# Five of eight sets of weight sums made on VectorE in the last stage, not by accumulating DMAs

## The chip, the cores and the metric

The kernel runs on one core of a Trainium2 chip. The metric is the device time of one execution in microseconds (us). A core has TensorE (PE), VectorE (DVE), ScalarE (ACT), GpSimd (POOL) and SyncE (SP); each works through its own instructions in order. All DMAs are issued here by SP, a few by POOL and ACT, and run on the core's 16 DMA engines.

## The reference

```python
def _moe_ref(x, expert_emb, tau, w1, w2):        # x: 2304 tokens of 512, from the attention
    ...
    for e in range(E):                            # 8 experts, one for each token
        mask = expert_idx == e
        h = np.maximum(x[mask] @ w1[e], 0.0)      # 512 to 1024
        out[mask] = gate_w[mask, None] * (h @ w2[e])
    return out

def _moe2_ref(x, w_in, w_out):                    # w_in 512x2048, w_out 2048x512
    h = x @ w_in
    g = h * (1.0 / (1.0 + np.exp(-h)))
    return g @ w_out
```

An attention (32 pairs of batch and head, 576 tokens each) makes the tokens, a layer of experts follows (`_moe_ref`), and a feed-forward layer with two matrices ends it (`_moe2_ref`). All is fp32.

## The kernel before

PE reads an fp32 matrix as two parts, high and low, so that a product is three matmuls: high by high, high by low, low by high (`three`, lines 798 to 800). The parts are made by a copy on ACT (high) and a subtraction on DVE (low). This goes for weights and for activations.

**The slots.** After the attention come 22 expert slots, each for up to 128 tokens of one expert. SP loads the expert's weights, 4 MB when the expert changes, in pieces of 1536 and 512 KB (`fetch`, line 811, into `raw`). ACT and DVE split them (`split`, lines 847 and 848). PE turns the tokens of the next slot (`xturn`, four transposes into `pxt`, line 868), multiplies (`mm1`, then `mm2` of the slot before) and turns the result (`hturn`; the copies `hh` and `hl`, lines 852 and 855). POOL gathers the tokens of later slots (`gather`, line 833).

**Weight sums.** The last stage multiplies by `w_in` in a scheme of seven products instead of eight for a pair of column tiles q (0 to 7) and a block of 576 tokens. For it each pair needs seven matrices, each 256x128 and held as 128x256: four are tiles of the converted `w_in`, three are sums of these. They lie side by side in DRAM, in `sscr[q]`, [128, 7, 256], 896 KB. The first five pairs' tiles are converted during the attention, the last three during slots 7 to 16, with their loads and stores on POOL's queue (`cload`, `cwork`, `cstore`). `keep_weights` stores a tile, some of it broadcast to several places. Then `add_weights` (line 193) adds one place onto others by an accumulating DMA from DRAM to DRAM on POOL's queue. `ADDS` lists 21 of these: 13 of three places (384 KB) and 8 of one (128 KB). Slot s issues two of them, from slot 8 on. For the last three pairs DVE makes one sum on the way (`both`, line 224), and a store spreads it (line 184).

**The last stage.** It is cut in 32 units u, unit u for pair q = u % 8 and token block u // 8. PE runs in unit u the products 1, 5, then 4 of the unit before, 6, 3 of the unit before, 2 and 7 (`unit`); each is six matmuls of 128x288. Products 1, 6, 7, 4 collect in PSUM bank A, where ACT copies them out (`keep`). Products 5 and 3 collect in bank C and 2 in B, where DVE adds them onto the copied tile (`join`), and SP stores the result (`hstore`, into `hd`). `join(u, 5)` reads bank C before product 3 of u adds to it, so PE waits for it. A dictionary `todo` holds what is done after product n in unit u: `at(u, n, task)`; the order in which it runs is the order on each engine. Before the change:

- `wfetch(q)` loads `sscr[q]` as it is into the low half of the weight tile (SP, line 983): q = 0 to 3 in the last slots into `wb`, 4 and 5 ahead of unit 0 and 6 and 7 in units 1 and 2, into `wbr`. 
- `whigh(q)` (ACT, after product 6 of unit q-2) and `wlow(q)` (DVE, after product 5 of unit q-1) split it. 
- `xfetch`, `xscale` and `xprep` prepare the tokens of the next block from unit 2 on: a load of `yt` (by SP or as a gather by POOL, line 1002), a scale by the gate on DVE for the first two tiles (line 1010), and four transposes on PE (line 1019). The first of them stand after product 1 of units 2 and 3.
- `oload`, `cwork`, `cstore` convert the 16 tiles of `w_out` in units 6 to 24.
- The branch `rest`, for experts with more tokens than the slots hold, stands ahead of unit 5 and is not taken.

A down stage (`w_out`) ends the kernel.

Of the kernel before, what the change touches and what calls it, by code (L numbers as in the profile page):

```python
# [9 lines left out]
F32 = mybir.dt.float32  # L10
# [4 lines left out]
ALU = mybir.AluOpType  # L15
# [4 lines left out]
P = 128  # L20
# [12 lines left out]
NJ = FF2 // P  # L33
TN = 288
NJP = NJ // 2
# [9 lines left out]
CA = 10  # L45
# [3 lines left out]
SQ = [{}, {1: (0, 1), 3: (2, 3), 5: (4,)}, {1: (0, 1), 3: (2, 3), 5: (4,)}, {i: (i,) for i in range(NB)}]  # L49
RANK = (1, 0)  # L50
WARM = (10, 14)
BITS = [-1, 0, 1, 2, 3, 4, 5, 6, 7, 11, 12, 13, 14, 15, 19, 20, 21, 22, 23, 24]
# [14 lines left out]
def moe_kernel(ctx, tc, qk, v, w_phi, emb, tau, w1, w2, win, wout, out):  # L67
    nc = tc.nc
# [9 lines left out]
    yd = dram.tile([NT + 2 * P, DM], F32, name="yd")  # L78
    sscr = [dram.tile([P, 7, 256], F32, name=f"sscr{i}") for i in range(NJP)]
    woscr = [dram.tile([P, 2, DM], F32, name=f"woscr{i}") for i in range(NJP)]  # L80
# [89 lines left out]

    def keep_weights(i, c, rw, dma=nc.sync):
        half, j = divmod(i, NJ)
        q, odd = divmod(j, 2)
        c = c.bitcast(F32)
        if half:
            dma.dma_start(out=woscr[q][:, odd, :], in_=c)
        elif i < CA and odd:
            dma.dma_start(out=sscr[q][:, 6, :], in_=c[:, 0:256])
            dma.dma_start(out=sscr[q][:, 2:6, :], in_=c[:, 256:512].unsqueeze(1).to_broadcast([P, 4, 256]))
        elif odd:  # L180
            both = rw.rearrange("p f t -> p (f t)")[:, 0:256].bitcast(F32)
            dma.dma_start(out=sscr[q][:, 6, :], in_=c[:, 0:256])
            dma.dma_start(out=sscr[q][:, 2, :], in_=c[:, 256:512])
            dma.dma_start(out=sscr[q][:, 3:6, :], in_=both.unsqueeze(1).to_broadcast([P, 3, 256]))
        else:
            dma.dma_start(out=sscr[q][:, 0:2, :], in_=c.rearrange("p (a f) -> p a f", a=2))

    ADDS = [(q, n) for n in (6, 0, 1) for q in range(CA // 2)] + [(5, 0), (6, 0), (5, 1), (7, 0), (6, 1), (7, 1)]

    def add_weights(q, n):  # L190
        a, b = {6: (3, 6), 0: (4, 7), 1: (5, 6)}[n]
        src = sscr[q][:, n:n + 1, :]
        nc.gpsimd.dma_start(out=sscr[q][:, a:b, :], in_=src.to_broadcast([P, b - a, 256]) if b - a > 1 else src,
                            accum_op=ALU.add)

    def narrow(rw, c, eng, i):
# [16 lines left out]
        for f in (shift, scale) if eng is nc.scalar else (scale, shift):  # L213
# [5 lines left out]
                                       op1=ALU.bitwise_xor)  # L219
        if CA <= i < NJ and i % 2:  # L220
            yield
            a, b = c.bitcast(F32)[:, 0:256], c.bitcast(F32)[:, 256:512]
            both = rw.rearrange("p f t -> p (f t)")[:, 0:256].bitcast(F32)
            nc.vector.tensor_tensor(out=both, in0=a, in1=b, op=ALU.add)

    class Convert:
# [13 lines left out]
        def work(self, i):  # L240
            c = self.done(i)
            yield from narrow(self.h[i], c, nc.vector, i)
            self.h[i] = c, self.h[i]

        def store(self, i):
            keep_weights(i, *self.h.pop(i))

# [9 lines left out]
    def phase_all(ctx):  # L257
# [517 lines left out]
        pools = {}  # L775
# [174 lines left out]
        def cstore(i, dma):  # L950
            rw, c, todo = J.pop(i)
            next(todo, None)
            keep_weights(i, c, rw, dma)

# [25 lines left out]
        def wfetch(q):  # L980
            if q < 4:
                wspace(q)
            nc.sync.dma_start(out=W[q][1].bitcast(F32), in_=sscr[q].rearrange("p a f -> p (a f)"))

        def whigh(q):
            nc.scalar.copy(out=W[q][0], in_=W[q][1].bitcast(F32))

        def wlow(q):
            hi, lo = W[q]
            nc.vector.tensor_tensor(out=lo, in0=lo.bitcast(F32), in1=hi.bitcast(F32), op=ALU.subtract)  # L990

# [432 lines left out]
        for s in range(1, NSF + 1):  # L1424
# [9 lines left out]
            if s < NSF:  # L1434
                if s + 2 < NSF:
                    gather(s + 2)
                for q, n in ADDS[max(2 * s - 16, 0):max(2 * s - 14, 0)]:
                    add_weights(q, n)
                for k in range(4):
# [48 lines left out]
            if s == NSF - 1:  # L1488
                xfetch(1, 0)
                xfetch(1, 1)  # L1490
                wfetch(3)
            if s < NSF:
# [15 lines left out]
        def at(u, n, *task):  # L1508
            todo.setdefault((u, n), []).append(task)

        htile(0, (0, 0))
        for q in range(4, NJP):
            wspace(q)
        wfetch(4)
        wfetch(5)
        def plan():
            for q in range(2, NJP):
                at(q - 2, 6, whigh, q)
                at(q - 1, 5, wlow, q)
            at(1, 4, wfetch, 6)  # L1520
            at(2, 4, wfetch, 7)
            for k in range(1, NT // (2 * TN)):
# [13 lines left out]
                for v, n, name in ((7, 5, "T1n"), (7, 6, "T2n"), (7, 2, "B21"), (7, 7, "T3"), (8, 4, "T4"), (8, 3, "B22")):  # L1536
                    at(u + v, n, xsplit, k, name)
            units = [u for u in range(6, 25) if u not in (7, 15, 23)]
            assert len(units) == NJ
# [19 lines left out]
        for u in range(NUNIT):  # L1559
            if u == NJP - 3:  # L1560
                more = nc.values_load(regs[0:1, 2, NSF:NSF + 1], min_val=0, max_val=NT + P)
                with tc.If(more < NT + P):
                    rest()
            unit(u, todo, EARLYP)
# [53 lines left out]
```

## Time and profile before

| | |
|---|---|
| median of 3 runs | 927.96 us (927.53 to 928.4) |
| the profiled execution, whole | 928.01 us |
| its span on the core | 926.3 us |
| PE busy | 900.8 us |
| DVE, ACT, POOL busy | 618.4, 583.1, 267.7 us |

The span goes from the first to the last instruction on the core; 1.7 us of the execution lie around it. An engine is busy while it runs an instruction; in order to see what it waits for in the rest of the time, one reads the list of its waits (for whom, how long, how often) and the timeline, where a wait stands in brackets behind the instruction that ended it.

### The profile page before, as it was taken

How to read it: one execution, taken by the hardware profiler on the slowest of the kernel's cores; microseconds unless marked ns; L12 is line 12 of the kernel's file. 1: busy time of each engine (PE TensorE's matmuls, PEld its weight loads, DVE VectorE, ACT ScalarE, POOL GpSimd, SP SyncE). 2: the span in 40 equal slices, each digit the busy share in tenths (PEclk: the TensorE clock that was granted, in tenths of full speed). 3: DMA queues.
4: the chain of work that ended last, by engine and by line, in shares of the span. 5: the costliest groups of instructions: out<-in, count | busy, mean ns of one | idle time of the engine just before them, and what ended most of it. 6: DMA issues, size and time to landing. Idle time of an engine off the chain costs nothing. (4 is left out here: it accounts for less than half of the span.)

```text
span 926.3 us, 15648 instructions
## 1 busy us (share of the span) xinstructions
PE 900.8 (97%) x5567; PEld 787.3 (85%) x5567; DVE 618.4 (67%) x967; ACT 583.1 (63%) x948; POOL 267.7 (29%) x236
## 2 busy tenths in 40 slices
PE   8999999999999999979999989999999999999996
PEld 6999999987767788858878889999999888888885
DVE  7888898986798999959988857676756122222220
ACT  6877888745978898859888755343456344444331
POOL 6887887712200406416230021101000110000000
PEclk9999999999999999989999999999999999999999
DMA  6455353449455738995698585777776844444420
GB/s 181 111 155 169 93 180 93 112 134 363 159 184 195 252 90 203 356 335 142 179 324 322 190 287 182 232 261 232 241 255 209 209 114 119 120 113 114 119 63 23
DMA packets 136739, 171.69 MB, mean 185 GB/s; under 512 B 34664, under 2 KB 97768, under 8 KB 136656
## 3 DMA queue, kind: packets, MB, share of 16 engines
q1 hardware_dynamic: 124064, 144.06, 48.8%
q0 software_dynamic: 12512, 26.55, 10.9%
q8 instruction: 45, 0.74, 0.3%
q14 instruction: 38, 0.31, 0.1%
q10 hardware_dynamic: 80, 0.03, 0.0%
HBM read 170.87 MB, written 52.04 MB: 241 GB/s over the span
## 5 line engine op out<-in xcount | busy, mean ns | idle before, releaser
L848 DVE TENSOR_TENSOR wl<-raw,wh 128x1024 fp32r<-128x1024 f32 (+1 forms) x166 | 187.7, 1173 | 31.6 <-ACT wh L847 26.8
L847 ACT CAST wh<-raw 128x1024 fp32r<-128x1024 f32 (+1 forms) x166 | 161.4, 1026 | 27.5 <-DMA raw<-w 15.3
L1169 DVE TENSOR_TENSOR hlt<-gt,hlt 128x1024 fp32r<-128x1024 f32 x34 | 41.7, 1226 | 146.4 <-ACT hlt L1168 146.4
L1093 ACT COPY ht<-puA 128x288 f32<-128x288 f32 x128 | 51.0, 400 | 92.4 <-PE puA L800 81.4
L799 PE MATMUL po<-wob,hlt 128*128 128x512 f32 x272 | 108.5, 399 | 0.0
L798 PE MATMUL po<-wob,hlt 128*128 128x512 f32 x272 | 107.2, 394 | 0.0
L800 PE MATMUL po<-wob,hlt 128*128 128x512 f32 x272 | 106.6, 392 | 0.0
L434 POOL TENSOR_TENSOR kl<-ke,kh 128x640 fp32r<-128x640 f32 x52 | 84.1, 1639 | 30.7 <-issue 23.0
L1189 ACT COPY os<-po 128x512 f32<-128x512 f32 x17 | 10.0, 588 | 108.4 <-PE po L800 108.4
L484 PE MATMUL pnx<-kv,qp 128*128 128x73 f32 x640 | 76.6, 275 | 0.0
L484 PEld LDWEIGHTS pnx<-kv,qp 128*128 128x128 f32 x640 | 74.1, 192 | 0.1
L1190 POOL DMA_INDIRECT out<-os,oidx x18 | 17.6, 976 | 179.1 <-ACT os L1189 168.6
L798 PE MATMUL ph<-wh,xh 128*128 128x512 f32 x166 | 67.1, 404 | 0.0
L800 PE MATMUL ph<-wh,xl 128*128 128x512 f32 x166 | 65.1, 392 | 0.8 <-DVE xl L855 0.8
L799 PE MATMUL ph<-wl,xh 128*128 128x512 f32 x166 | 64.7, 390 | 0.0
L1100 DVE TENSOR_TENSOR ht<-puC,ht 128x288 f32<-128x288 f32 x64 | 29.0, 453 | 52.7 <-PE puC L800 39.1
L395 DVE TENSOR_REDUCE m<-pqk 128x10 f32<-128x1280 f32 x32 | 47.5, 1485 | 24.3 <-PE pqk L389 22.9
L798 PEld LDWEIGHTS po<-wob,hlt 128*128 128x128 f32 x272 | 51.0, 188 | 13.3
L800 PEld LDWEIGHTS po<-wob,hlt 128*128 128x128 f32 x272 | 51.1, 188 | 12.3
L419 ACT ACTIVATE ke<-d 128x640 f32<-128x640 f32 x52 | 38.3, 737 | 36.7 <-DVE d L396 36.7
L799 PEld LDWEIGHTS po<-wob,hlt 128*128 128x128 f32 x272 | 51.0, 188 | 11.6
L389 PE MATMUL pqk<-wbd,zh 128*128 128x256 f32 (+1 forms) x320 | 59.0, 283 | 0.8 <-DVE d L396 0.6
(403 smaller groups left out, 2443.8 us busy)
## 6 DMA issues: line engine op xcount, KB each, us to landing
raw<-w SPq DMA_DIRECT2D x44, 1536.0 KB
raw<-w SPq DMA_DIRECT2D x44, 512.0 KB
hd<-ht SPq DMA_DIRECT2D x124, 144.0 KB
gt<-hd SPq DMA_DIRECT2D x15, 1024.0 KB
z<-qk SPq DMA_DIRECT2D x32, 288.0 KB
wo<-wout SPq DMA_DIRECT2D x16, 512.0 KB
yd<-ys SPq DMA_DIRECT2D x23, 256.0 KB
raw<-win SPq DMA_DIRECT2D x10, 512.0 KB
```

What stands on the lines that cost most here:

```text
L389: nc.tensor.matmul(out=pqk[0:r, c * 256:(c + 1) * 256], lhsT=z[:, c * P:c * P + r], rhs=wbd[:, j].rearrange("p h f -> p (h f)"), start=(i ...
L395: nc.vector.tensor_reduce(out=m, in_=pv, axis=AX.X, op=ALU.max, apply_absolute_value=True)
L419: nc.scalar.activation(out=ke, in_=kd, func=AF.Exp, scale=1.0 - 2.0 * s)
L434: nc.gpsimd.tensor_tensor(out=kl[:, :, s, :], in0=st.pop(("ke", g, s)), in1=kh[:, :, s, :].bitcast(F32), op=ALU.subtract)
L484: nc.tensor.matmul(out=pn[:, c, 0:73], lhsT=qp[:, s, c * P:(c + 1) * P], rhs=kv[:, s, 0:73], start=(s == 0), stop=(s == 1))
L798: nc.tensor.matmul(out=o, lhsT=ah, rhs=bh, start=first, stop=False, skip_group_check=more)
L799: nc.tensor.matmul(out=o, lhsT=ah, rhs=bl, start=False, stop=False, skip_group_check=more)
L800: nc.tensor.matmul(out=o, lhsT=al, rhs=bh, start=False, stop=last, skip_group_check=more)
L847: nc.scalar.copy(out=hi[:, 0:n], in_=sl[:, 0:n])
L848: nc.vector.tensor_tensor(out=lo[:, 0:n], in0=sl[:, 0:n], in1=hi[:, 0:n].bitcast(F32), op=ALU.subtract)
L1093: nc.scalar.copy(out=htile(u, at), in_=BK[u, "A"])
L1169: nc.vector.tensor_tensor(out=lo, in0=g, in1=hi.bitcast(F32), op=ALU.subtract)
```

## The change

Pairs 0 to 2 (`QD = 3`) keep their sums in DRAM, by nine accumulating DMAs, one a slot from slot 8 to slot 16. For pairs 3 to 7 only the four tiles are stored ([128, 4, 256], 512 KB, without broadcasts). In units 0 to 4 SP loads them into a tile `ws` in SBUF (two buffers), and DVE makes the sums there with four additions of 128x256 (`wsum`). `whigh` and `wlow` read from `ws` and write the weight tile. `wfetch(3)` leaves the last slots, and `wfetch(4)` and `(5)` leave the place ahead of unit 0. The tiles of `w_out`, which use the same two buffers, are converted in units 8 to 25, and the branch stands ahead of unit 7.

```diff
+QD = 3
...
-    sscr = [dram.tile([P, 7, 256], F32, name=f"sscr{i}") for i in range(NJP)]
+    sscr = [dram.tile([P, 7 if i < QD else 4, 256], F32, name=f"sscr{i}") for i in range(NJP)]
...
-        elif i < CA and odd:
+        elif q >= QD:
+            if odd:
+                dma.dma_start(out=sscr[q][:, 0, :], in_=c[:, 0:256])
+                dma.dma_start(out=sscr[q][:, 3, :], in_=c[:, 256:512])
+            else:
+                dma.dma_start(out=sscr[q][:, 1:3, :], in_=c.rearrange("p (a f) -> p a f", a=2))
+        elif odd:
             dma.dma_start(out=sscr[q][:, 6, :], in_=c[:, 0:256])
             dma.dma_start(out=sscr[q][:, 2:6, :], in_=c[:, 256:512].unsqueeze(1).to_broadcast([P, 4, 256]))
-        elif odd:
-            both = rw.rearrange("p f t -> p (f t)")[:, 0:256].bitcast(F32)
-            dma.dma_start(out=sscr[q][:, 6, :], in_=c[:, 0:256])
-            dma.dma_start(out=sscr[q][:, 2, :], in_=c[:, 256:512])
-            dma.dma_start(out=sscr[q][:, 3:6, :], in_=both.unsqueeze(1).to_broadcast([P, 3, 256]))
...
-    ADDS = [(q, n) for n in (6, 0, 1) for q in range(CA // 2)] + [(5, 0), (6, 0), (5, 1), (7, 0), (6, 1), (7, 1)]
+    ADDS = [(q, n) for n in (6, 0, 1) for q in range(QD)]
...
-        if CA <= i < NJ and i % 2:
-            yield
-            a, b = c.bitcast(F32)[:, 0:256], c.bitcast(F32)[:, 256:512]
-            both = rw.rearrange("p f t -> p (f t)")[:, 0:256].bitcast(F32)
-            nc.vector.tensor_tensor(out=both, in0=a, in1=b, op=ALU.add)
...
         def wfetch(q):
-            if q < 4:
+            if q < QD:
                 wspace(q)
-            nc.sync.dma_start(out=W[q][1].bitcast(F32), in_=sscr[q].rearrange("p a f -> p (a f)"))
+                nc.sync.dma_start(out=W[q][1].bitcast(F32), in_=sscr[q].rearrange("p a f -> p (a f)"))
+            else:
+                W["r", q] = pools["ul"].tile([P, 2048], F32, tag="ws", name="ws", bufs=2)
+                nc.sync.dma_start(out=W["r", q][:, 0:1024], in_=sscr[q].rearrange("p a f -> p (a f)"))
+
+        def wsum(q):
+            r = W["r", q].rearrange("p (a f) -> p a f", a=8)
+            for o, a, b in ((4, 3, 0), (7, 1, 0), (5, 4, 1), (6, 5, 2)):
+                nc.vector.tensor_tensor(out=r[:, o], in0=r[:, a], in1=r[:, b], op=ALU.add)
+
+        def wsource(q):
+            return W["r", q][:, 256:] if q >= QD else W[q][1].bitcast(F32)
...
         def wlow(q):
             hi, lo = W[q]
-            nc.vector.tensor_tensor(out=lo, in0=lo.bitcast(F32), in1=hi.bitcast(F32), op=ALU.subtract)
+            nc.vector.tensor_tensor(out=lo, in0=wsource(q), in1=hi.bitcast(F32), op=ALU.subtract)
...
-                for q, n in ADDS[max(2 * s - 16, 0):max(2 * s - 14, 0)]:
-                    add_weights(q, n)
+                if 8 <= s < 8 + len(ADDS):
+                    add_weights(*ADDS[s - 8])
...
-                wfetch(3)
...
-        wfetch(4)
-        wfetch(5)
         def plan():
-            for q in range(2, NJP):
-                at(q - 2, 6, whigh, q)
-                at(q - 1, 5, wlow, q)
-            at(1, 4, wfetch, 6)
-            at(2, 4, wfetch, 7)
+            at(0, 6, whigh, 2)
+            at(1, 5, wlow, 2)
+            for q in range(QD, NJP):
+                at(q - 3, 3, wfetch, q)
+                at(q - 3, 7, wsum, q)
+                at(q - 2, 3, whigh, q)
+                at(q - 2, 7, wlow, q)
...
-            units = [u for u in range(6, 25) if u not in (7, 15, 23)]
+            units = [u for u in range(8, 26) if u not in (15, 23)]
...
-            if u == NJP - 3:
+            if u == NJP - 1:
```

The rows below are instructions in the order of each engine's program, with line, operation, output and inputs; `sscr_67` to `sscr_74` are `sscr[0]` to `sscr[7]`, and `hd_83` is `hd` of the first token block.

DVE in the first units, before. `L1100` is `join` (of `puB`: product 2; of `puC`: products 5 and 3), `L990` is `wlow`, `L1010` is `xscale`:

```order
L1100 TENSOR_TENSOR ht<-puB,ht 128x288
L1100 TENSOR_TENSOR ht<-puC,ht 128x288
L990 TENSOR_TENSOR wb<-wb 128x1792
L1100 TENSOR_TENSOR ht<-puC,ht 128x288
L1100 TENSOR_TENSOR ht<-puB,ht 128x288
L1010 TENSOR_SCALAR yt<-yt,gate_s 128x512
L1100 TENSOR_TENSOR ht<-puC,ht 128x288
L990 TENSOR_TENSOR wb<-wb 128x1792
```

The same place after the change, where `L1108` is `join`, `L986` is `wsum`, `L998` is `wlow` and `L1018` is `xscale`:

```order
L1108 TENSOR_TENSOR ht<-puB,ht 128x288
L986 TENSOR_TENSOR ws<-ws 128x256 x4
L1108 TENSOR_TENSOR ht<-puC,ht 128x288
L998 TENSOR_TENSOR wb<-wb 128x1792
L1108 TENSOR_TENSOR ht<-puC,ht 128x288
L1108 TENSOR_TENSOR ht<-puB,ht 128x288
L998 TENSOR_TENSOR wb<-ws,wb 128x1792
L986 TENSOR_TENSOR ws<-ws 128x256 x4
L1018 TENSOR_SCALAR yt<-yt,gate_s 128x512
L1108 TENSOR_TENSOR ht<-puC,ht 128x288 x2
L1108 TENSOR_TENSOR ht<-puB,ht 128x288
L998 TENSOR_TENSOR wbr<-ws,wbr 128x1792
```

A `wsum` now stands ahead of each `join` of product 5, and ahead of `xscale` where there is one.

SP from the end of the slots into unit 2, before:

```order
L936 DMA yd<-ys 128x512
L983 DMA wbr<-sscr_71 128x1792
L983 DMA wbr<-sscr_72 128x1792
L1106 DMA hd_83<-ht 128x288 x3
L983 DMA wbr<-sscr_73 128x1792
L1106 DMA hd_83<-ht 128x288 x4
L983 DMA wbr<-sscr_74 128x1792
```

And after the change, up to unit 3:

```order
L933 DMA yd<-ys 128x512
L981 DMA ws<-sscr_70 128x1024
L1114 DMA hd_83<-ht 128x288 x4
L981 DMA ws<-sscr_71 128x1024
L1114 DMA hd_83<-ht 128x288 x4
L981 DMA ws<-sscr_72 128x1024
L1114 DMA hd_83<-ht 128x288 x4
L981 DMA ws<-sscr_73 128x1024
```

One fetch goes out ahead of the units, and each later one behind the four stores of a unit, the last of which is that of product 3's `join`.

POOL in slots 10 to 12, before. `L833` gathers tokens, `L169` loads a tile of `w_in`, `L182` to `L186` store converted tiles, `L193` are the accumulating DMAs:

```order
L193 DMA sscr_71<-sscr_71 128x3x256
L193 DMA sscr_67<-sscr_67 128x3x256
L182 DMA sscr_72<-x 128x256
L183 DMA sscr_72<-x 128x256
L184 DMA sscr_72<-x 128x3x256
L169 DMA x<-win 128x4x256
L833 DMA xg<-xd,gidx 128x512
L193 DMA sscr_68<-sscr_68 128x3x256
L193 DMA sscr_69<-sscr_69 128x3x256
L186 DMA sscr_73<-x 128x512
L833 DMA xg<-xd,gidx 128x512
L193 DMA sscr_70<-sscr_70 128x3x256
```

After the change:

```order
L195 DMA sscr_69<-sscr_69 128x3x256
L180 DMA sscr_72<-x 128x256
L181 DMA sscr_72<-x 128x256
L170 DMA x<-win 128x4x256
L830 DMA xg<-xd,gidx 128x512
L195 DMA sscr_67<-sscr_67 128x3x256
L183 DMA sscr_73<-x 128x512
L830 DMA xg<-xd,gidx 128x512
L195 DMA sscr_68<-sscr_68 128x3x256
```

One accumulating DMA a slot in place of two, and no store of three places.

## Rows read from the trace of the kernel before

**Rows 1.** The page's first part: busy us, share, instructions per engine.

```profile
PE 900.8 (97%) x5567; PEld 787.3 (85%) x5567; DVE 618.4 (67%) x967; ACT 583.1 (63%) x948; POOL 267.7 (29%) x236
```

**Rows 2.** Waits of PE: waiter and releaser, total us, times, longest.

```profile
PE py L798 <- ACT hh L852: 6.2, 1, 6.2
...
PE pt L1019 <- DMA yt<-yd,yidx: 1.3, 1, 1.3
...
PE pt L1019 <- ACT xf L1025: 1.0, 1, 1.0
```

**Rows 3.** Timeline of PE, three slots: start, duration, operation, count, [wait].

```profile
391.16 0.60 PE L868 MATMUL pxt<-ident,xg 128*128 128x128 f32 x4
...
403.59 0.60 PE L868 MATMUL pxt<-ident,xg 128*128 128x128 f32 x4
...
424.87 0.60 PE L868 MATMUL pxt<-ident,xg 128*128 128x128 f32 x4
```

**Rows 4.** Timeline of ACT, its waits for expert weights in two slots.

```profile
409.24 0.62 ACT L847 CAST wh<-raw 128x512 fp32r<-128x512 f32 x1 [7.67 <-DMA raw<-w]
...
477.84 2.00 ACT L847 CAST wh<-raw 128x1024 fp32r<-128x1024 f32 x2 [1.89 <-DMA raw<-w]
```

**Rows 5.** Timeline of SP's queue: expert weights; `wbr` ahead of unit 0.

```profile
388.18 1.12 SPq L811 DMA_DIRECT2D raw<-w  x2
...
532.26 2.09 SPq L983 DMA_DIRECT2D wbr<-sscr  x2
```

**Rows 6.** Windows: busy per engine, granted clock, DMA share, GB/s.

```profile
356.00:417.00 61.00, 54.57 (x249) 43.34 (x248) 47.99 (x56) 43.92 (x64) 20.58 (x20) 0.94 1.07 322
410.40:413.00 2.60, 2.38 (x5) 1.47 (x6) 2.40 (x5) 2.60 (x5) 0.00 (x0) 0.50 1.06 369
...
538.00:544.00 6.00, 6.00 (x48) 6.00 (x48) 3.78 (x6) 3.54 (x8) 2.21 (x1) 1.00 0.97 356
...
545.00:552.00 7.00, 5.73 (x45) 5.52 (x44) 3.24 (x4) 4.71 (x9) 2.37 (x2) 1.00 0.89 288
```

**Rows 7.** DMA queues (packets, MB, share of engines); issues (KB, us to landing).

```profile
q1 hardware_dynamic: 124064, 144.06, 48.8%
q0 software_dynamic: 12512, 26.55, 10.9%
...
sscr<-sscr POOLq DMA_DIRECT2D x13, 384.0 KB, 10.9
...
yt<-yd,yidx POOLq DMA_INDIRECT x13, 4.5
```

**Rows 8.** Timeline of POOL: accumulating adds, the stretch's first and last.

```profile
353.21 2.68 POOL L193 DMA_DIRECT2D sscr<-sscr  x2
...
396.50 0.84 POOL L193 DMA_DIRECT2D sscr<-sscr  x1 [0.85 <-DMA sscr<-sscr]
```

**Rows 9.** Line 224 on DVE: count, ns min/median/max, first to last start.

```profile
L224 DVE TENSOR_TENSOR x<-x x3: 412/415/417, 367.7 to 458.8; 128x256 f32<-128x256 f32 x3
```

**Rows 10.** Timelines of SP and ACT at the start: a 288 KB load.

```profile
0.82 0.41 SPq L305 DMA_DIRECT2D z<-qk  x1
...
3.56 0.67 ACT L375 CAST zh<-z 128x576 fp32r<-128x576 f32 x1 [0.67 <-DMA z<-qk]
```

**Rows 11.** Timeline of DVE in units 1 and 2.

```profile
536.07 2.02 DVE L990 TENSOR_TENSOR wb<-wb 128x1792 fp32r<-128x1792 f32 x1
538.41 0.46 DVE L1100 TENSOR_TENSOR ht<-puC,ht 128x288 f32<-128x288 f32 x1 [0.33 <-PE puC L800]
...
539.65 0.48 DVE L1010 TENSOR_SCALAR yt<-yt,gate_s 128x512 f32<-128x512 f32 x1
```

**Rows 12.** Timeline of PE in units 1 and 2.

```profile
538.21 0.30 PE L798 MATMUL puB<-xcB,wb 128*128 128x288 f32 x1
...
540.61 0.60 PE L1019 MATMUL pt<-ident,yt 128*128 128x128 f32 x4
540.97 0.38 PE L798 MATMUL puC<-xcT1n,wb 128*128 128x288 f32 x1
```

More of the change, by code (lines that the diff above doesn't have):

```diff
@@ L169, in fetch_raw, with keep_weights @@
         q.dma_start(out=dst, in_=src.bitcast(I32))
-    def keep_weights(i, c, rw, dma=nc.sync):
+    def keep_weights(i, c, dma=nc.sync):
         half, j = divmod(i, NJ)
@@ L242, in work @@
             yield from narrow(self.h[i], c, nc.vector, i)
-            self.h[i] = c, self.h[i]
+            self.h[i] = c
         def store(self, i):
-            keep_weights(i, *self.h.pop(i))
+            keep_weights(i, self.h.pop(i))
         def step(self, g, first, last):
@@ L950, in cstore @@
         def cstore(i, dma):
-            rw, c, todo = J.pop(i)
-            next(todo, None)
-            keep_weights(i, c, rw, dma)
+            keep_weights(i, J.pop(i)[1], dma)
         HOOKS = [(s, n) for s in range(7, 17) for n in (1, 5, 7)]
@@ L980, in wfetch @@
         def wfetch(q):
-            if q < 4:
+            if q < QD:
                 wspace(q)
-            nc.sync.dma_start(out=W[q][1].bitcast(F32), in_=sscr[q].rearrange("p a f -> p (a f)"))
+                nc.sync.dma_start(out=W[q][1].bitcast(F32), in_=sscr[q].rearrange("p a f -> p (a f)"))
[8 more added lines that the diff above has]
+            return W["r", q][:, 256:] if q >= QD else W[q][1].bitcast(F32)
         def whigh(q):
-            nc.scalar.copy(out=W[q][0], in_=W[q][1].bitcast(F32))
+            if q not in W:
+                wspace(q)
+            nc.scalar.copy(out=W[q][0], in_=wsource(q))
         def wlow(q):
             hi, lo = W[q]
-            nc.vector.tensor_tensor(out=lo, in0=lo.bitcast(F32), in1=hi.bitcast(F32), op=ALU.subtract)
+            nc.vector.tensor_tensor(out=lo, in0=wsource(q), in1=hi.bitcast(F32), op=ALU.subtract)
         def tiles_of(k):
```

## The prediction

> **What bounds the kernel now.** I read the page's busy times first, then the waits of PE, then PE's timeline around each wait and the queues behind it. PE is busy for 900.8 of 926.3 us [rows 1]; no other engine passes 67%, so only what makes PE wait costs time. The list of PE's waits has one large entry: 6.2 us, once, for `hh` from ACT [rows 2]. Slot starts on PE (the four transposes into `pxt`) lie 12.43 us apart before it and 21.28 us across it [rows 3], so this one place loses 8.85 us: the wait of 6.2 and 2.6 more, most of it because PE came out of the wait at a granted clock of 0.50, its lower level of 1.2 GHz [rows 6]. ACT was late because it stood before the cast of a weight piece for 7.67 us, until 409.24 [rows 4]. That piece is the second load of the pair issued at 388.18 [rows 5], some 20 us before. From 356 to 417 the DMA engines were full: share 1.07, 322 GB/s [rows 6]. So in slots 9 to 13 the queue is the limit, and bytes taken from it there may be worth time on PE.
>
> Two smaller waits have the same cause. At 477.84 ACT waits 1.89 us for weights [rows 4] and PE then waits 1.0 for ACT's `xf` [rows 2]. In unit 3 PE waits 1.3 us for a gathered `yt` [rows 2], while the four `wbr` fetches of 896 KB, the first of which go out at 532.26 [rows 5], fill the engines (356 GB/s at a share of 0.97 [rows 6]).
>
> **What goes: traffic in the slots.** All traffic of the software queue took 10.9% of 926.3 us, 101 us, for 26.55 MB [rows 7]. The 21 accumulating adds are 13 of 393 KB and 8 of 131 KB, 6.16 MB; the other 20.4 MB at the plain queue's price (48.8% of 926.3 us for 144.06 MB, 3.14 us a MB [rows 7]) make 64 us. That leaves 37 us for the adds, 6 us a MB: 2.4 us of all 16 engines for a large add, 0.8 for a small one.
>
> In the stretch of adds from 353.21 to 396.50 [rows 8], three large adds before the load's issue at 388.18 fall away, and one broadcasting store of 384 KB (about 1.2 us by the plain price), so 3 x 2.4 + 1.2 = 8.4 us. From then to 396.50 there were two large and two small adds (6.4); now there are two large ones (4.8). In all the queue ahead of the load is shorter by 10.0 us. PE stops waiting when the load lands 6.2 us sooner or somewhat more. If all 10.0 count, the whole 8.85 is won; if half of them (other traffic flows in where the adds leave room), 5.0, about 1.4 us of wait stay, without a fall of the clock, and 7.4 is won. I take the middle, **-8.1**. The adds of slots 14 to 18 shrink alike, and I count the wait near 482 as gone: **-1.0** (bounds 0 and -1.0). The three adds of `both` on DVE (415 ns each [rows 9]) and their stores were no PE wait; nothing for them.
>
> **What goes in the units.** No 896 KB fetches there, so the gather lands in time: **-1.3** (bounds 0 and -1.3).
>
> **What comes in the units: a wait of DVE for a DMA, at the head of its queue.** `wsum(q)` waits for `ws(q)`. Behind it on DVE, in order, stand `xscale` (for units 2 and 3) and `join(u,5)`. PE's transposes of `yt` at the head of units 2 and 3 need `xscale`, and product 3 needs `join(u,5)`. And `ws(q+1)` is issued on SP only behind the `hd` store of `join(u,3)`, which needs product 3. This is a ring: product 3, join, store, fetch, four adds, then PE again. Five fetches, so one entry into the ring and four rounds.
>
> The price of a fetch, T, is the unknown. A load of 288 KB at the kernel's start is issued at 0.82 and used at 3.56: 2.74 us alone [rows 10]. 512 KB are 0.229 MB more, 0.64 us at 356 GB/s [rows 6]; an `hd` store of 144 KB goes out 0.46 us ahead and I give it 0.3. T = 3.7. Bounds: 2.74 (a smaller load, alone), and 4.5, the median landing of the `yt` gathers [rows 7].
>
> The Trainium skill, "DMA: Bandwidth & Descriptors", section "Anatomy of one DMA — SWDGE (gpsimd) path", gives a fixed 2.0 us and the bytes at 436 GB/s; that is 2.7 us for 288 KB, as this trace shows, and 3.2 us, an estimate from the page, for 512 KB.
>
> Other durations: a product 0.80 us and four transposes 0.36 (538.21, 540.61, 540.97 [rows 12]: three products, then the transposes); a join 0.46, `xscale` 0.48, `wlow` 2.02 [rows 11]; four adds of 128x256 at 0.42, 1.68 [rows 9]; about 0.2 from PE's end to a join and 0.46 for the store ahead of the fetch. Let E be the end of product 3 of unit u-1.
> - Entry: `ws(3)` is issued where the first `wbr` went, 532.26 [rows 5]; 3.7 + 1.68 + 0.46 end `join(0,5)` at 538.1. PE wants it at 537.41 (0.80 before 538.21 [rows 12]). Wait 0.7.
> - Round 1: `wlow(2)` now stands between `join(0,5)` and `join(0,3)`. It starts with product 3 and runs 2.02, so `join(0,3)` ends at E+1.7, not E+0.66. Fetch issued E+2.1, landed E+5.8, adds done E+7.5, `xscale` E+8.0. PE reaches the transposes three products after E, at E+2.4. Wait 5.6.
> - Round 2: `join(1,3)` ends E+0.66, fetch E+1.12, landed E+4.8, adds E+6.5, `xscale` E+7.0; PE is there at E+2.4. Wait 4.6.
> - Rounds 3 and 4, without `xscale`: `join(u,5)` ends at E+1.12+3.7+1.68+0.46 = E+6.96; PE wants it after six products and mostly one set of transposes, E+5.16. Wait 1.8 each.
>
> Sum **+14.5**. Each 0.1 us of T moves it by 0.5: at 2.74 it is 9.9 (the entry then costs nothing), at 4.5 it is 18.5.
>
> **The clock after these waits.** After 6.2 us PE stood at the lower level [rows 2, 6]; after the 1.3 us near 550 it stayed at 1.00 [rows 6]. Waits of 5.6 and 4.6 lie between, nearer to the first. A fall cost 2.4 us in slot 13 (8.85, less 6.2, less 0.2 of waiting behind it). I count one of the two, **+2.4**; bounds 0 and +4.8.
>
> Nothing else reaches PE, I believe: `whigh` and `wlow` keep count and size, the converted `w_out` tiles move by one or two units and have DVE's idle time as cover (33% over the kernel [rows 1]), and the branch costs the same in unit 7 as in unit 5. Without that cover a late tile would show only behind unit 26, at the 512 KB fetches of `woscr`.
>
> **Sum.** The profiled run took 928.01 us, 0.05 over the median, so both serve: 928.0 - 8.1 - 1.0 - 1.3 + 14.5 + 2.4 = **934.5 us**.
>
> **Rivals.**
> - *The fetch is quick and the clock holds* (the other side: not slower). At T = 3.2, midway between 2.74 and 3.7, the ring costs 12.0, without a fall: 928.0 - 10.4 + 12.0 = 929.6. At T = 2.74: 927.5; with the whole 8.85 in the slots 926.8. It decides from T of about 3.2 down. For it: the load of 288 KB [rows 10]; against it: the waits are then still 5.1 and 4.1 us, and the `hd` stores share the engines. By the page's 3.2 us and one fall of the clock the sum would be 932.0.
> - *The slots don't gain* (the change does not do there what it says): the expert weights alone (4 MB for each change of expert, in loads of 1536 and 512 KB) fill the queue, and the load lands later than about 406.0, less than 3.2 us sooner. Then some 3 us or more of waiting and a fall of the clock may stay: gain 3.5 in place of 8.1, 939. For it: share 1.07 over 61 us [rows 6], of which I remove 10 us of work.
> - *The ring is slower*: T = 4.5 as the gathers [rows 7], and both long waits drop the clock: 928.0 - 10.4 + 18.5 + 4.8 = 940.9.
> - *The ring is not felt*: something lets `ws` go out sooner or PE pass, and the slots' gain stands alone, 918 to 922. The order on DVE and SP speaks against it.
>
> **How the numbers follow.** 0.2%, 1.9 us, is about what a measurement of this kernel can tell from no change: 926.1 to 929.8. The forecast's own case (930 to 937.5, T from 3.2 with a fall to 4.2) 0.64; quick fetch without a fall, 926.5 to 929.8, 0.15; the slots don't gain 0.09; slower ring 0.06; ring not felt 0.06. Faster 0.07, same 0.14, slower 0.79. The range 928 to 939 leaves out part of the quick case, the ring not felt, and the slowest ends, together about 0.2.
>
> **What would show it.** Right: `pxt` starts in slot 13 about 12.4 to 14 us apart; no wait of PE for `hh` over 2 us; DVE waits for `ws` from DMA, some 1 to 4 us a round, before L986; PE waits for DVE's `yt` before two sets of transposes, 5.6 and 4.6 us, and for `join` behind them by 1.8 twice; a granted clock of 0.5 after one of the long waits; no wait for the gathered `yt` in unit 3. Wrong: T outside 3.2 to 4.2 (each 0.1 is 0.5 us), a clock that falls never or twice, or a load in slot 12 that still lands after 406.

## The result and the profile after

The changed kernel takes 940.74 us (median of 4 runs, 940.09 to 943.11), the kernel before 928.18 (4 runs on the same chip). The ratio is 1.0134, with a 95% interval of 1.0107 to 1.0162: slower by 12.6 us. The forecast was slower, 934.5, with a range of 928 to 939; the direction is right, the time 1.7 us outside the range. The profiled execution took 940.23 us, its span is 938.5.

PE's waits in the changed kernel (us in total, times, longest), against [rows 2]:

```profile
PE pt L1027 <- DVE yt L1018: 9.9, 2, 5.3
PE puC L795 <- DVE ht L1108: 4.1, 4, 1.7
PE puA L795 <- ACT ht L1101: 1.9, 4, 0.8
PE puA L795 <- PEq L1569: 1.7, 1, 1.7
```

The waits for `hh`, for the gathered `yt` and for `xf` are gone from the head of the list. New are two for the scaled `yt` on DVE, those for `join`, and one at the branch (PEq is PE's own sequencer, line 1569 the branch).

PE's timeline over the slots (against [rows 3]) and then in the units:

```profile
403.90 0.60 PE L865 MATMUL pxt<-ident,xg 128*128 128x128 f32 x4
...
417.66 0.60 PE L865 MATMUL pxt<-ident,xg 128*128 128x128 f32 x4
...
529.30 0.40 PE L795 MATMUL puC<-xcB,wb 128*128 128x288 f32 x1 [0.45 <-DVE ht L1108]
...
538.10 1.11 PE L1027 MATMUL pt<-ident,yt 128*128 128x128 f32 x4 [5.34 <-DVE yt L1018]
...
550.31 1.09 PE L1027 MATMUL pt<-ident,yt 128*128 128x128 f32 x4 [4.56 <-DVE yt L1018]
...
563.56 0.40 PE L795 MATMUL puC<-xcB,wb 128*128 128x288 f32 x1 [1.73 <-DVE ht L1108]
571.44 0.40 PE L795 MATMUL puC<-xcB,wbr 128*128 128x288 f32 x1 [1.62 <-DVE ht L1108]
...
581.93 0.37 PE L795 MATMUL puA<-xcA,wbr 128*128 128x288 f32 x1 [1.74 <-PEq L1569]
```

The slot that took 21.28 us takes 13.76. Then come the entry and the four rounds of the ring, in the order in which the prediction has them: 0.45, 5.34, 4.56, 1.73, 1.62. The four transposes behind the long waits take 1.11 and 1.09 us where they took 0.60 [rows 12].

The cause of each long wait is read on SP and DVE. SP issues a fetch of `ws`:

```profile
523.49 0.39 SPq L981 DMA_DIRECT2D ws<-sscr  x1
...
531.93 0.48 SPq L981 DMA_DIRECT2D ws<-sscr  x1
...
544.29 0.38 SPq L981 DMA_DIRECT2D ws<-sscr  x1
```

and DVE waits for it, adds, and only then scales `yt`:

```profile
527.32 1.56 DVE L986 TENSOR_TENSOR ws<-ws 128x256 f32<-128x256 f32 x4 [3.54 <-DMA ws<-sscr]
...
536.09 1.55 DVE L986 TENSOR_TENSOR ws<-ws 128x256 f32<-128x256 f32 x4 [2.25 <-DMA ws<-sscr]
537.56 0.48 DVE L1018 TENSOR_SCALAR yt<-yt,gate_s 128x512 f32<-128x512 f32 x1
...
548.22 1.55 DVE L986 TENSOR_TENSOR ws<-ws 128x256 f32<-128x256 f32 x4 [1.56 <-DMA ws<-sscr]
549.69 0.48 DVE L1018 TENSOR_SCALAR yt<-yt,gate_s 128x512 f32<-128x512 f32 x1
```

From issue to use a fetch takes 3.8, 4.2 and 3.9 us, and 4.0 and 3.8 in the last two rounds. The scales end at 538.0 and 550.2; PE's transposes start 0.1 us behind.

Windows of the changed kernel behind the two long waits (columns as in [rows 6]):

```profile
538.10:542.00 3.90, 3.90 (x20) 3.90 (x21) 0.31 (x1) 0.57 (x2) 0.95 (x1) 0.60 0.29 91
...
550.30:554.00 3.70, 3.69 (x16) 3.70 (x17) 0.23 (x1) 0.59 (x1) 0.95 (x1) 0.50 0.30 71
```

The granted clock is 0.60 and 0.50: it fell in both waits.

PE runs the same 5567 matmuls in the same order in both kernels, so each can be set beside itself. How far the changed kernel is ahead (-) or behind (+), at starts taken from the two timelines, in one profiled execution of each:

| PE's instruction | before | after | shift | what lies between |
|---|---|---|---|---|
| slot start (`pxt`) | 403.59 | 403.90 | +0.3 | |
| slot start, the next | 424.87 | 417.66 | -7.2 | slot 13 |
| first `pt` in the last slots | 482.26 | 473.92 | -8.3 | the wait of 1.0 for `xf` |
| `po`, end of the slots | 525.66 | 516.94 | -8.7 | |
| product 3 of unit 0 | 537.41 | 529.30 | -8.1 | entry |
| `pt`, unit 2 | 540.61 | 538.10 | -2.5 | round 1, wait |
| product 3 of unit 1 | 543.44 | 542.40 | -1.0 | half clock |
| `pt`, unit 3 | 546.64 | 550.31 | +3.7 | round 2, wait |
| gathered `pt`, unit 3 | 550.90 | 555.24 | +4.3 | half clock +1.95, gather's wait -1.3 |
| product 3 of unit 3 | 557.26 | 563.56 | +6.3 | round 3 |
| product 3 of unit 5 | 569.27 | 577.54 | +8.3 | round 4, a join |
| product 1 of unit 7 | 571.66 | 581.93 | +10.3 | the branch |
| PE's end | | | +11.4 | later units |
| the span | 926.3 | 938.5 | +12.2 | what is left behind PE |

### The profile page after: what moved, and what is told of

Its sections match the earlier page's. It is cut to its first block, busy times and chain, and to the rows that moved or that the text cites. A ratio compares the mean times of both kernels' runs of the same rounds, so it can differ in the third digit from the quotient of the medians.

```text
span 938.5 us, 15637 instructions
## 1 busy us (share of the span) xinstructions
PE 904.0 (96%) x5567; PEld 789.8 (84%) x5567; DVE 624.2 (67%) x984; ACT 584.5 (62%) x948; POOL 246.2 (26%) x221
## 5 line engine op out<-in xcount | busy, mean ns | idle before, releaser
L1108 DVE TENSOR_TENSOR ht<-puC,ht 128x288 f32<-128x288 f32 x64 | 29.0, 453 | 51.9 <-PE puC L797 44.4
L1010 POOL DMA_INDIRECT yt<-yd,yidx x13 | 12.9, 991 | 187.3 <-PE pt L1027 160.7
```

## The experiments

Each time stands beside the kernel before on the same chip, since that one's medians lie between 926.4 and 928.2.

**The scale ahead of the sums.** Only DVE's order changes:

```diff
-                    at(u + v, m, xscale, k, n)
+                    at(*((u + v - 1, 2) if n < 2 else (u + v, m)), xscale, k, n)
```

> The changed kernel, with the two scales of yt moved ahead of the sums on DVE (after product 2 of units 1 and 2, not after product 1 of units 2 and 3). Theory (DVE holds the scale behind sums that wait for a fetch): PE's two waits for yt (5.3 and 4.6) go, and PE waits instead for the join behind the sums, about 2.7 and 1.6 us; no fall of the clock. 940.7 - 5.6 - 3.4 = 931.7, 930.5 to 933.5. Rival (the fetch and the ring alone set the pace and the place of the scale does not matter): the same waits at another instruction, 939 to 941.

Measured: 931.73 us beside 926.49 (ratio 1.0055, 1.0038 to 1.0072); by the two ratios that is 7 us under the changed kernel. PE's waits for `yt` are gone, and those for `join` have grown from 4.1 us in all to 8.7:

```profile
PE puC L795 <- DVE ht L1108: 8.7, 6, 2.7
```

The clock stayed at 1.00 in the units. So some 5 us of waiting and all of the half clock came from where the scale stood, not from the fetch as such. (The times of the experiments are medians; the waits are those of one profiled execution each.)

**The fetch earlier.**

```diff
-                at(q - 3, 3, wfetch, q)
+                at(q - 3, 5 if q > QD else 3, wfetch, q)
```

> The changed kernel, with the fetches of pairs 4 to 7 issued after product 5 instead of after product 3 of the same unit, so that they stand behind the store of the join of product 5 and no longer behind that of product 3. Theory (a ring through the store of product 3's join): fetches go out some 2 to 3 us sooner, PE waits about 3.0 and 3.5 us for yt and 0.6 us in the two rounds behind, and at most one fall of the clock stays: 932 to 936. Rival (DVE is late with its own work and not for the fetch): within 1.5 us of 940.7.

Measured: 935.40 beside 926.49 (1.0091, 1.0073 to 1.0108). PE waits 6.6 us in two waits for `yt`, the longest 3.7, and 1.9 in all for `join`. The last sums find their fetch landed:

```profile
534.89 1.55 DVE L986 TENSOR_TENSOR ws<-ws 128x256 f32<-128x256 f32 x4 [0.60 <-DMA ws<-sscr]
545.40 1.55 DVE L986 TENSOR_TENSOR ws<-ws 128x256 f32<-128x256 f32 x4
```

The ring through the store is open, as the theory has it, and the time is in its range. But at 545.40 DVE waits for no DMA and PE still waits 2.9 us in that round: the low part and the sums stand ahead of the scale and take DVE's time. So the landing was about 1.7 of the 4.6 us in that round, DVE's own work ahead of the scale the rest. The theory's "at most one fall of the clock" failed: it fell behind both waits for `yt`, and once more behind PE's 2.1 us at the branch.

**Sums one unit later**, with the scale ahead:

```diff
-                at(q - 3, 7, wsum, q)
-                at(q - 2, 3, whigh, q)
-                at(q - 2, 7, wlow, q)
+                at(q - 2, 7, wsum, q)
+                at(q - 1, 1, whigh, q)
+                at(q - 1, 5, wlow, q)
```

> The changed kernel, with the scales moved ahead as in the run above them and the sums, the high and the low parts of pairs 3 to 7 made one unit later each (sums after product 7 of unit q-2, high after product 1 and low after product 5 of unit q-1); the fetches stay where they are, so each has a whole unit to land. Theory: no wait of DVE for ws, no long wait of PE in units 0 to 4; the slots' gain stays: 940.7 - 14.4 of waits - 3.4 of half clock = 922.9, 921 to 924.5, faster than both kernels. Rival (DVE has too much to do in these units, 1.5 us of sums and 2.0 of low parts in 5.2 us): it becomes the bound there, 926 to 932.

Measured: 924.72 beside 926.49 (0.998, 0.9966 to 0.9995), a little faster than the kernel before and, by the ratios, 14 us under the changed one, with the same work done; that is 0.2 us over the theory's range. DVE waits for no `ws` any more and the clock stays at 1.00 in the units; of `join` 0.4 us of waiting is left. At the head of PE's list stands the branch:

```profile
PE puA L795 <- PEq L1569: 2.8, 1, 2.8
```

**The slots, in parts.** First, in the kernel before, only the adds:

```diff
-    ADDS = [(q, n) for n in (6, 0, 1) for q in range(CA // 2)] + [(5, 0), (6, 0), (5, 1), (7, 0), (6, 1), (7, 1)]
+    ADDS = [(q, n) for n in (6, 0, 1) for q in range(3)]
...
-                for q, n in ADDS[max(2 * s - 16, 0):max(2 * s - 14, 0)]:
-                    add_weights(q, n)
+                if 8 <= s < 8 + len(ADDS):
+                    add_weights(*ADDS[s - 8])
```

> The kernel before, with twelve of its 21 accumulating DMAs left out and the other nine issued one a slot from slot 8; its stores, fetches and units stay as they were. The sums of pairs 3 to 7 are therefore incomplete. Theory (the accumulating DMAs delay the weight load of slot 12): PE's 6.2 us wait for hh, the half clock behind it and the 1.0 us wait near 482 go, the 1.3 us wait for the gathered yt and the units stay: 928.2 - 8.7 = 919.5, 918.5 to 921. Rival (the plain stores in place of broadcasts, or the fetch of pair 3 that left the last slots, made the slots faster): little of it shows here, 924 to 928.

Measured: 922.08 beside 926.49 (0.995, 0.9933 to 0.9966). The wait for `hh` is 3.6 us, not gone, and the clock fell behind it:

```profile
PE py L798 <- ACT hh L852: 3.6, 1, 3.6
```

ACT, with its wait for the weight load in that run:

```profile
406.69 0.62 ACT L847 CAST wh<-raw 128x512 fp32r<-128x512 f32 x1 [8.42 <-DMA raw<-w]
```

The load is there at 406.69 in place of 409.24 [rows 4], 2.6 us sooner, where the prediction gave these adds 8.8 us of the queue. The time, 4.6 us less by the ratio, lies between the theory's range and the rival's.

Then only the store, with the step on DVE. The adds go two a slot again, up to slot 15; the last six, of slots 15 to 18, are left out here too:

```diff
-            dma.dma_start(out=sscr[q][:, 3:6, :], in_=both.unsqueeze(1).to_broadcast([P, 3, 256]))
...
-    ADDS = [(q, n) for n in (6, 0, 1) for q in range(CA // 2)] + [(5, 0), (6, 0), (5, 1), (7, 0), (6, 1), (7, 1)]
+    ADDS = [(q, n) for n in (6, 0, 1) for q in range(CA // 2)]
...
-        if CA <= i < NJ and i % 2:
-            yield
-            a, b = c.bitcast(F32)[:, 0:256], c.bitcast(F32)[:, 256:512]
-            both = rw.rearrange("p f t -> p (f t)")[:, 0:256].bitcast(F32)
-            nc.vector.tensor_tensor(out=both, in0=a, in1=b, op=ALU.add)
```

> The kernel before without the sum on DVE (both) and its spreading store of 384 KB, but with the first 15 accumulating DMAs two a slot as before (the last six, in slots 15 to 18, are left out; sums of pairs 5 to 7 incomplete, their fetches read stored places twice). Adds alone had taken 2.6 us of PE's wait for hh, adds and store together 5.9. Theory (the store and its step hold POOL, whose next load of 512 KB then falls on the weight load, more than the bytes of the adds do): the wait falls to 2 to 4 us here, 922 to 925. Rival (only the bytes count, 384 KB of 5 MB): a wait of 5 us or more, 925.5 to 928.

Measured: 924.28 beside 926.40 (0.9972, 0.9957 to 0.9987), but the wait for `hh` stays at 5.4 us:

```profile
PE py L791 <- ACT hh L845: 5.4, 1, 5.4
```

The load is there at 408.93, 0.3 us sooner. That is no gain that can be told from nothing: in the kernel with the late edits alone (below), whose slots are those of the kernel before, ACT has it at 408.45 and PE waits 5.4 us as well:

```profile
408.45 0.62 ACT L847 CAST wh<-raw 128x512 fp32r<-128x512 f32 x1 [7.37 <-DMA raw<-w]
```

So the rival holds in this slot, by its wait and not by its time. The waits of 1.0 and 1.3 us near 482 and 550 are not in this profile; whether the 2.6 us that the ratio gives come from the store or from the six adds is not shown.

In this run and the next one the last three pairs are fetched from the places that are stored:

```diff
-            nc.sync.dma_start(out=W[q][1].bitcast(F32), in_=sscr[q].rearrange("p a f -> p (a f)"))
+            for a, b, n in ((0, 0, 7),) if q < CA // 2 else ((0, 0, 3), (3, 0, 3), (6, 6, 1)):
+                nc.sync.dma_start(out=W[q][1].bitcast(F32)[:, a * 256:(a + n) * 256],
+                                  in_=sscr[q][:, b:b + n, :].rearrange("p a f -> p (a f)"))
```

Then both, adds and store, by the edits above (the adds as in the first of these runs):

> As the run with twelve adds left out of the kernel before, and now the sum on DVE (both) and its spreading store of 384 KB for the last three pairs are left out too; their fetches read the stored places twice, so that they move as many bytes. Sums of pairs 3 to 7 are incomplete. Leaving out the adds alone took 2.6 of PE's 6.2 us wait. Theory (the store and the step on DVE, which POOL waits for at the head of its queue, move POOL's later loads into the time of the weight load): the rest of the wait goes as in the changed kernel, hh under 1 us, 928.2 - 8.7 - 0.7 = 918.8, 917.5 to 920.5. Rival (it is the plain stores of pairs 3 and 4 in the attention, or the fetch of pair 3 that left the slots): as with the adds alone, a wait of 3 to 4 us and 921 to 923.

Measured: 919.46 beside 926.97 (0.9927, 0.9904 to 0.9949). No wait for `hh` stands in the list any more, which is headed by

```profile
PE puA L791 <- ACT ht L1088: 1.3, 2, 0.8
```

and ACT starts that cast at 402.44, no longer held by the load:

```profile
402.44 0.62 ACT L840 CAST wh<-raw 128x512 fp32r<-128x512 f32 x1 [5.37 <-PE ph L793]
```

In these profiles the two edits together bring the cast forward by 6.8 us, more than 2.6 and 0.3 added up, so PE's wait for `hh` went only with both. The times don't say so: by the ratios the parts gain 4.6 and 2.6 us, both together 6.8, which adds up within the intervals. The profile of this run is the quickest of its four executions; another took 922.62 us at a mean granted clock of 0.995 (0.998 in the profiled one). By what way the two edits may help each other isn't settled: in the run with the adds alone POOL issues its next load of `w_in` at 372.78, behind the store, and without the store at 366; but with the store alone taken out that load moves to 366 too and the cast comes no sooner.

**The branch, in three kernels.** The changed kernel with the branch ahead of unit 6:

```diff
-            if u == NJP - 1:
+            if u == NJP - 2:
```

> The changed kernel with the branch ahead of unit 6, not 7. In the kernel before it stood ahead of unit 5 and PE's branch took 0.7 us, hidden in PE's queue; ahead of unit 7 it took 3.4 us and PE stood for 1.7. Theory (the price hangs on where the branch lies in PE's code): either the 1.7 us go, 938.5 to 939.3, or another price between 0 and 3 us stands there; the waits of units 0 to 4 stay as they are. Rival (the time is a wait for the other engines at the branch in unit 7): gone wherever PE does not run ahead, and the same 1.7 us here.

Measured: 939.85 beside 926.97 (1.0131, 1.0111 to 1.0151), the changed kernel's time. PE stands for 1.6 us again, now some instructions behind the branch:

```profile
577.00 0.40 PE L797 MATMUL puC<-xcT1n,wbr 128*128 128x288 f32 x1 [1.64 <-issue]
```

So there is a price at another place, the theory's second case. Against the rival speaks the kernel before, where PE leaves its branch at 558.95 and ACT, SP and DVE come to theirs from 560.47 to 560.99: PE does not wait for them. The clock fell a third time in this run, behind a wait of 2.2 us in round 3, so the equal time gives no clean price.

The kernel before, with only the late edits (`w_out` in units 8 to 25, branch ahead of unit 7):

```diff
-            units = [u for u in range(6, 25) if u not in (7, 15, 23)]
+            units = [u for u in range(8, 26) if u not in (15, 23)]
...
-            if u == NJP - 3:
+            if u == NJP - 1:
```

> The kernel before with one edit of the change alone: the tiles of w_out converted in units 8 to 25 and the branch ahead of unit 7 (DMAs, sums and order of units 0 to 4 as before). Theory (the branch ahead of unit 7 makes PE stand, and the later tiles cost a little): 1.7 to 2.0 us at the branch and up to 1 us later, 929.8 to 931 against 928.2. Rival (PE stood at the branch because the waits of units 0 to 4 had let the queues run dry): within 0.5 us of the kernel before.

Measured: 931.98 beside 926.40 (1.0053, 1.0034 to 1.0072). The two late edits cost 4.9 us by the ratio, more than the 3 at most that the theory gave them. The profiled execution, 929.11 us, is the quickest of seven. In it PE stands for 3.1 us at the branch,

```profile
PE puA L798 <- PEq L1562: 3.1, 1, 3.1
```

and comes out of it at the lower clock:

```profile
571.00:574.00 3.00, 3.00 (x15) 3.00 (x14) 0.00 (x0) 0.96 (x2) 1.90 (x2) 0.50 0.36 105
```

Beside the kernel before, instruction by instruction, this place costs 4.8 us (3.2 of standing, 1.6 at the lower clock) and the later units 0.6. This falls against the rival: no wait of units 0 to 4 had run the queues dry. In this kernel, whose slots and early fetches are those of before, the waits of 1.0 near 482 and of 1.3 near 550 [rows 2] are absent too, as in all three runs on the slots. So they can be missing without the change.

The changed kernel without any branch, and without the code behind it, which these inputs don't use:

```diff
-            if u == NJP - 1:
-                more = nc.values_load(regs[0:1, 2, NSF:NSF + 1], min_val=0, max_val=NT + P)
-                with tc.If(more < NT + P):
-                    rest()
```

> The changed kernel without the branch and the code behind it (left out, not taken with these inputs). Theory: 2.0 us of the changed kernel's loss stand at the branch ahead of unit 7: 940.7 - 2.0 = 938.7, 937.5 to 939.5, and the waits of units 0 to 4 as before. Rival: PE's stand at the branch is hidden by other waits, 940 to 941.

Measured: 942.85 beside 927.60 (1.0174, 1.0151 to 1.0197), not faster. PE's stand at the branch is gone, but the waits in the ring are 5.6 and up to 2.7 us, and the clock is low a third time, in unit 5:

```profile
575.90:579.40 3.50, 3.50 (x16) 3.50 (x16) 1.04 (x3) 1.08 (x1) 0.00 (x0) 0.51 0.39 126
```

In that round the fetch took 4.9 us from issue to use, where the changed kernel's took 3.8:

```profile
568.80 0.32 SPq L981 DMA_DIRECT2D ws<-sscr  x1
...
573.71 1.56 DVE L986 TENSOR_TENSOR ws<-ws 128x256 f32<-128x256 f32 x4 [1.98 <-DMA ws<-sscr]
```

The forecast for this run failed: it took the rest of the kernel to stay as it was. Beside the changed kernel, instruction by instruction, this run is 5.4 us behind just ahead of unit 7 (1.2 of it from a wait for `hh` in the slots, most of the rest from the ring and the clock) and 3.5 behind it. So the branch's 1.9 us came back where it had stood, and other waits took more. Without the ring the branch's price shows clean, in the kernel with later sums and the same lines left out:

> The run with later sums, without the branch and the code behind it (for experts with more tokens than the slots hold, not taken with these inputs; left out). Theory: its profile showed PE standing 2.8 us at the branch and 3.1 us lost there; these go: 924.7 - 3.1 = 921.6, 920.5 to 922.5. Rival (a kernel with this many waits removed loses the time elsewhere behind unit 7): 923.5 to 925.

Measured: 921.10 beside 927.60 (0.994, 0.9924 to 0.9956). By the two ratios (0.998 and 0.994) the branch costs that kernel about 0.4%, 3.7 us; its profile had shown 3.1, and 3.0 come back at that place in this one.

**Two attempts at a faster kernel**, both with all the work of the changed kernel. The later sums moved a unit forward, so that the branch can stand ahead of unit 6:

```diff
+        wfetch(QD)
+        wfetch(QD + 1)
...
-                at(q - 3, 3, wfetch, q)
-                at(q - 2, 7, wsum, q)
-                at(q - 1, 1, whigh, q)
-                at(q - 1, 5, wlow, q)
+                if q > QD + 1:
+                    at(q - 4, 3, wfetch, q)
+                at(q - 3, 7, wsum, q)
+                at(q - 2, 1, whigh, q)
+                at(q - 2, 5, wlow, q)
...
-            if u == NJP - 1:
+            if u == NJP - 2:
```

> The run with later sums, moved one unit forward: pairs 3 and 4 fetched ahead of unit 0, each further pair one unit sooner than in the changed kernel; sums after product 7 of unit q-3, high part after product 1 and low part after product 5 of unit q-2; the scales ahead of the sums; the branch ahead of unit 6. All the work of the changed kernel is done. Theory: no wait of DVE for ws and no long wait of PE; the slots' gain, the gather's 1.3 us and, where the branch is cheap, all of it: 928.2 - 8.7 - 1.3 + 0.5 = 918.7; 917.5 to 922 with the branch's price open. Rival (low parts and sums crowd DVE in unit 1, where two low parts follow each other): PE waits 1 to 3 us in units 1 and 2, 920 to 924.

Measured: 925.31 beside 926.97 (0.998, 0.9968 to 0.9993), over both ranges. The rival's wait is seen: PE waits 1.2 us for `yt` behind two low parts in a row,

```profile
535.09 0.66 PE L1027 MATMUL pt<-ident,yt 128*128 128x128 f32 x4 [1.19 <-DVE yt L1018]
```

and 1.5 us behind the branch. With one low part moved to product 7:

```diff
-                at(q - 2, 5, wlow, q)
+                at(q - 2, 5 if q > QD else 7, wlow, q)
```

> The run one unit ahead with one low part moved: that of pair 3 after product 7 of unit 1, behind the scale, and no longer back to back with that of pair 2. All the work of the changed kernel is done. Theory: PE's wait of 1.2 us for yt in unit 2 goes and the 1.6 us behind the branch stay, 922.5 to 924.5, faster than both kernels. Rival (DVE is full in unit 1 wherever the low part stands): the wait turns up at product 3, 925 to 926.

Measured: 925.41 beside 926.40 (0.9986, 0.9973 to 0.9998). The theory's time failed; the rival's came. The wait of 1.2 us for `yt` is gone from unit 2, but smaller ones took its place: 0.9 in all for `join` (0.5 before), 0.5 for `yt` in unit 3 (0.3 before), and 0.9 more for ACT's copies out of bank A; behind the branch 1.2 us are left. The time is the same within the intervals. Of this run, the one before it and the later sums none is told apart from the others; each is faster than the kernel before by 0.1 to 0.2%.

## Where the prediction was right, and which step failed

**The slots: -8.7, forecast -9.1 (8.1 and 1.0).** The size is right in the profile, its working is not. I priced each large add at 2.4 us of the queue and added up; twelve adds fewer, which I gave 8.8 us of the queue, brought the load 2.6 us forward, the store nothing that can be told from chance, both together the cast 6.8. The -1.0 near 482 is not the change's: it is missing in the kernel whose slots are untouched as well. And the run with both edits alone gains 6.8 us of time, not 8.7. That the sum came out is in part luck.

**The gather: -1.3, as forecast in size,** but likewise gone in kernels that keep the 896 KB fetches. It is no gain of the change that these runs can show.

**The ring: +14.3, forecast +14.5.** The steps fit one by one: 0.6, 5.6, 4.7, 2.0 and 1.4 of shift against 0.7, 5.6, 4.6, 1.8 and 1.8. A fetch took 3.8 to 4.2 us where I had 3.7, and four sums 1.47 where I had 1.68; that these two errors cancel is luck, and in two other runs one fetch took 4.9. The 3.2 us that I had worked out from the Trainium skill, "DMA: Bandwidth & Descriptors", section "Anatomy of one DMA — SWDGE (gpsimd) path", is too little here: that sum fits the lone load of 288 KB, but its fit is of DMAs that POOL issues, and SP issues these. A store goes out just ahead of each fetch; that this is what makes them longer is not shown. The runs with the scale ahead, the earlier fetch and the later sums show the mechanism: each cuts one link, and the waits change as each link would have it.

**The clock: +3.4, forecast +2.4.** I counted one fall of two; both waits dropped it, at 1.5 and 1.95 us.

**The step that failed: "the branch costs the same in unit 7 as in unit 5".** I had put it at nothing, though its move stood in the diff and no row showed a branch at another place. PE stands there for 1.7 us, and the place costs 2.0 us in the profiled execution; less those 2.0 the measured time would be 938.7, within the range. Taken out of the changed kernel, the branch gave back 1.9 us at that place, though that run as a whole was no faster; out of the kernel with later sums, 3.0 there and 3.7 of its time. In the kernel before, the late branch cost 4.8 at that place, and with the late `w_out` 4.9 of the time. So the price is shown, and it differs between kernels. What PE seems to stand for, a load of instructions that ends after the branch begins, is read from the traces in the last section. With this step goes "nothing else reaches PE": a join in unit 5 cost 0.55, later units 1.1, and 0.8 lies behind PE's end. The run with the late edits alone lost 0.6 of that 1.1 in the later units too; the rest isn't explained. Together: 0.4 - 0.2 + 1.0 + 2.0 + 0.55 + 1.1 + 0.8 = 5.7 us, which is the 940.2 of the profiled execution less 934.5.

The rivals: the quick fetch that lets the clock hold did not come, nor the slots that gain nothing. The slower ring's 940.9 lies beside the measured 940.7 by luck: its two falls of the clock came, its fetch of 4.5 us did not. That the ring is felt followed from the order on DVE and SP, as the prediction had it.

## What to carry to other kernels

When work is put at the head of an in-order engine's queue to wait for a transfer, list all that stands behind it, not just the next consumer: here a scale of 0.48 us moved ahead of the sums took back 7 of the 12.6 us. Where the transfer's issue itself hangs on what the waiting engine lets go, the wait returns each round; one unit of distance between fetch and use ended it, with the same work done. Price each edit of a diff by a kernel that has it alone, the harmless ones too: a branch moved by two units, with the `w_out` tiles that moved with it, cost almost 5 us here. And price by times as well as by one profile: a wait of 1.0 or 1.3 us that is gone after a change may be gone without it.

## What the runs showed of the hardware

PE's branch instruction has no fixed price. Instructions of the branch's line in the kernel before (count, ns min/median/max, start):

```profile
L1562 PEldq COMPARE_BRANCH  x1: 685/685/685, 558.3 to 558.3; - x1
```

and in the changed kernel, where the other four engines' branches take 50 to 72 ns:

```profile
L1569 PEldq COMPARE_BRANCH  x1: 3372/3372/3372, 578.4 to 578.4; - x1
```

In the kernel with the late edits alone it took 4132 ns, and ahead of unit 6 only 353 ns, but then PE stood 1.64 us some instructions later. The DMA records show what ends with the stand. The page counts 45 loads of instructions, 16 KB each, on queue q8 (packets, MB, share):

```profile
q8 instruction: 45, 0.74, 0.3%
```

One of them lies within PE's branch in the changed kernel (the window 578.40 to 581.77), and none in the kernel before, where it is done ahead of the branch (556.60 to 557.60):

```profile
q8 instruction: 1, 0.02, 1.9%
...
q8 instruction: 1, 0.02, 5.7%
```

| kernel | branch starts | load of 16 KB | PE goes on | after the load's end |
|---|---|---|---|---|
| before | 558.26 | 556.61 to 557.52 | 558.95 | 1.43 |
| changed | 578.40 | 579.41 to 580.42 | 581.77 | 1.35 |
| later sums | 562.02 | 563.01 to 564.05 | 565.41 | 1.36 |
| late edits alone | 566.26 | 568.06 to 569.02 | 570.39 | 1.37 |
| branch ahead of unit 6 | 572.64 | 574.61 to 575.57 | 577.00 | 1.43 |

("PE goes on" is the end of the branch; with the branch ahead of unit 6 it is the matmul behind the stand.) In all twelve profiled kernels with a branch PE goes on 1.3 to 1.4 us after such a load ends. So PE seems to stand for instructions that are not there yet, and the place of the branch matters by when that load goes out. This is a reading of times that fall together; no run moved the load alone, and what sets its start is open.

A wait of PE need not be as long as the 6.2 us of [rows 2] for the clock to fall. It was at 0.50 behind waits of 3.7 us (the earlier fetch):

```profile
536.90:540.00 3.10, 3.10 (x14) 3.10 (x15) 0.30 (x1) 0.37 (x1) 0.94 (x1) 0.50 0.52 170
```

and of 2.9 and 3.1 us. It had also fallen behind one of 2.7 us in the changed kernel without a branch, 2.2 (the branch ahead of unit 6, round 3) and 2.1 (the branch of the run with the earlier fetch). Behind 2.73 and 2.65 us (the scale ahead) and 2.80 us (the branch with later sums) it stayed at 1.00. So of waits from 2.1 to 2.8 us some drop it and some don't.
